# Folding the second model's weights with three products of f16 halves instead of one in fp32, with a redrawn order

## The chip, the cores and the metric

The kernel runs on one core of a Trainium2 chip. The metric is device time in microseconds (us). The kernel before takes 1667.03 us (median of three runs, 1666.88 to 1668.13). The core has five instruction streams: PE (matrix products, with weight loads that can run beside them), DVE (vector work), ACT (activations and scaled copies), POOL (general vector work without access to the accumulators) and SP (which here issues all DMAs).

## The reference

Two attention models on separate inputs, whose outputs are put side by side. Both have 2048 positions, width 1024 and 32 heads of 32.

```python
def _A_ref(x, wq, wk, wv, wo, beta):        # four segments of 512
    q, k, v = x @ wq, x @ wk, x @ wv          # by head
    ...
    for s in range(N):
        p = softmax(qs @ ks.T * scale + mask); a_dot = p @ vs
        a_mem = (phi(qs) @ M) / (phi(qs) @ z + 1e-6)
        outs.append(g * a_mem + (1 - g) * a_dot)
        M, z = M + phi(ks).T @ vs, z + phi(ks).sum()
    return o @ wo

def _B_ref(x, wqkv, w_phi, wo):
    qkv = (x @ wqkv) ...
    pq = einsum("bhsd,hdf->bhsf", q, w_phi)   # per head, 32 by 32
    pk = einsum("bhsd,hdf->bhsf", k, w_phi)
    phi_q = concat(softmax(pq), softmax(-pq))
    phi_k = concat(softmax(pk), softmax(-pk))
    kv, z = einsum(phi_k, v), phi_k.sum()
    o = (phi_q @ kv) / (phi_q @ z + 1e-6)
    return o @ wo

return concatenate([_A_ref(...), _B_ref(...)], axis=-1)
```

In the second model q and k enter only through q @ w_phi and k @ w_phi. So the kernel multiplies w_phi into the weights once: wqkv's q and k columns, head by head, times the head's 32x32 feature map. That is the fold.

## The kernel before, in words

**Precision.** Nearly all products run in f16. A matrix is scaled by its own maximum and split into an upper half (the value rounded to f16) and a lower half (the rest, f16 again); a product is then three matmuls, upper by upper, upper by lower and lower by upper. A split is a scaled copy on ACT and a subtraction on DVE or POOL (`halves`, `forms`).

**Stages.** From the start to about 43 us the first segment of the first model and its first weights are loaded, scaled and split. Then 32 units of the first model's attention follow (`produce(u)`, `attend(u)` and the shared `values(u)`): projections of a head group, row maxima, scores, masks, values and the memory. Alongside, unit by unit, the second model's weights are prepared: `fold` in the units, `sizes_v` and `weights_v` for its value weights. From about 805 us the second model runs, first its keys and values (to about 1180 us), then its queries and output, with the first model's output weights prepared meanwhile; the last eight blocks, from about 1520 us, are the first model's output projection.

**The fold** (L1135 to L1221). The feature map stands in a tile of its own, `phib` (128 x 8 x 128, fp32): eight groups of four heads, each a 128x128 matrix with the four 32x32 maps on its diagonal and zeros elsewhere. POOL clears it at L1110 (after all other clears) and four DMAs at L1112 fill the diagonals. The q and k weights are eight blocks (m = 0 to 7) of four parts of 128x512. Block 0 is folded at the start, in `fold(-1)`: four fp32 matmuls a part (L1180). The other 28 parts are folded one per unit: a DMA loads the part into a stage buffer `st` (tag st, two buffers, L1147), four fp32 matmuls of 128 columns multiply it with `phib` (L1214), and DVE scales the result into the block `quad` (L1217). `size` (L1150) loads the parts of the next block into the same two buffers and takes its largest absolute row sums on ACT (L1156); with the feature map's own sums (`phs`, L1117) they bound the folded weights and give the scale `sif`. After the fourth part, `cut` builds seven sums and differences of the block, splits them and writes them to DRAM.

**The order.** Every instruction is written down as an operation with an engine, a duration, what it reads and writes, and a priority (`op`, L143). `run` (L207) then fixes the order of all engines by playing the operations through: at each step the engine that can start first takes the ready operation with the smallest priority. [...] Where PE would wait long, filler matmuls whose result nobody uses are put in (`fill`, L194, seen as L379 in the profile). `nudge` (L92) shifts the priorities of each run of 60 operations by a hash of a number in the table `NUDGE`, so the table draws one order among many. SP issues DMAs in the order so found; each engine works through its list in order.

**The end.** For each of eight blocks seven groups of twelve matmuls (L1718) fill three accumulators; `keep` (L1727) copies one out on ACT, `store` (L1739) adds another on DVE and sends it with a DMA (L1744). The last is a copy of 128x512 on ACT and one DMA of 256 KB.

Of the kernel before, what the change touches and what calls it, by code (L numbers as in the profile page):

```python
# [8 lines left out]
F32 = mybir.dt.float32  # L9
F32R = mybir.dt.float32r  # L10
F16 = mybir.dt.float16
# [34 lines left out]
NUDGE = {0: 820989, 2: 102852, 3: 529656, 4: 266905, 5: 924189, 6: 435410, 9: 911235, 12: 450738, 13: 124130, 14: 669972,  # L46
# [261 lines left out]
def tile_kernel(ctx: ExitStack, tc: tile.TileContext, ax, aw, awv, awo, beta, bx, bwqk, bwv, bphi, bwo, out):  # L308
# [65 lines left out]
    for t in vlb:  # L374
        nc.gpsimd.memset(t[:, :, :, 32:33], 0.0)
        nc.gpsimd.memset(t[:, :, :, 65:66], 1.0)
# [758 lines left out]
    def fold(n, prio, dep=()):  # L1135
# [14 lines left out]
        def size(m, i, qd=None):  # L1150
            if i == 0:
                sizes[m] = (G.buf("a", [128, 4], F32, "twf", 1), G.buf("a", [128, 2], F32, "sif", 2))
# [648 lines left out]
```

## Time and profile before

| what | us |
|---|---|
| median of the runs | 1667.03 |
| the profiled execution | 1667.0 |
| its span, first to last instruction | 1665.2 |
| POOL busy | 1060.6 |
| ACT busy | 1111.6 |

The profile is of one execution. "Busy" of an engine is the time that its instructions take by the trace; a matmul's end is modelled, and neighbouring matmuls overlap, so distances from start to start tell more about PE than durations. A row of a group gives the line, the engine, the operation, output and inputs, the shapes and how many there were, then the busy time, the mean of one in ns, and the idle time of the engine before them with what ended it.

### The profile page before, as it was taken

What the parts mean: (1) busy time and instruction counts of PE and PEld (TensorE: products, weight loads), DVE (VectorE), ACT (ScalarE), POOL (GpSimd) and SP (SyncE); (2) the same over time, 40 slices, a digit from 0 to 9 for tenths busy, and PEclk for the clock granted to TensorE, in tenths of its full rate; (3) what the DMA queues carried; (4) which work ended last, traced back from release to release, by engine and by line L of the source; (5) the groups of instructions that cost most, each with busy time, mean ns of one, the idle gap of its engine ahead of it and who ended that gap; (6) DMA issues with size and microseconds to landing.
All of it is one profiled execution on the core that took longest, in us unless ns stands there. A gap on an engine that the chain in (4) does not pass through costs nothing.

```text
span 1665.2 us, 35567 instructions
## 1 busy us (share of the span) xinstructions
PE 1644.1 (99%) x12922; PEld 964.4 (58%) x12922; DVE 1357.2 (82%) x3212; ACT 1111.6 (67%) x2044; POOL 1060.6 (64%) x1393
## 2 busy tenths in 40 slices
PE   8999999999999999999999999999999999999999
PEld 6666667667676666766754444445544444444444
DVE  6899989899897888897877898988997786975441
ACT  8798779868787777777865767645755464454431
POOL 4967577577777886967874454546699897640000
PEclk9999999999999999999999999999999999999999
DMA  7845556779456462756566354276466665753311
GB/s 238 238 137 155 158 156 170 204 203 240 115 160 163 132 180 90 193 194 176 154 203 260 121 197 170 85 257 248 171 153 152 169 176 158 216 149 136 121 57 64
DMA packets 265455, 279.68 MB, mean 168 GB/s; under 512 B 162752, under 2 KB 215744, under 8 KB 256704
## 3 DMA queue, kind: packets, MB, share of 16 engines
q1 hardware_dynamic: 265280, 277.42, 56.1%
q8 instruction: 101, 1.65, 0.4%
q14 instruction: 74, 0.61, 0.1%
HBM read 143.34 MB, written 85.00 MB: 137 GB/s over the span
## 4 chain that ended last, share of the span: by engine, by line
PE 80%; DVE 10%; ACT 3%; POOL 3%; issue 2%; DMA 1%; SPq 0%; DVEq 0%; ACTq 0%; POOLq 0%
PE proj L421 25%; PE proj L617 14%; PE misc L421 10%; PE proj L1718 5%; PE s L1033 4%; PE pv L1069 4%; PE s L940 3%; PE s L617 3%; PE s L1718 2%; PE misc L617 2%; PE pv L1654 2%; PE misc L1718 1%; PE misc L1214 1%; DVE mx L1319 1%; DVE s L946 1%
## 5 line engine op out<-in xcount | busy, mean ns | idle before, releaser
L421 PE MATMUL proj<-S,S 128*128 128x512 f16 (+1 forms) x2304 | 494.1, 343 | 0.7 <-ACT S L448 0.2
L421 PEld LDWEIGHTS <-S 128*128 128x128 f16 x3072 | 288.1, 98 | 160.4 <-issue 0.8
L617 PE MATMUL proj<-S,S 128*128 128x512 f16 x1488 | 342.7, 379 | 6.7 <-ACT cs L623 5.7
L617 PEld LDWEIGHTS <-S 128*128 128x128 f16 x1968 | 186.9, 98 | 219.9 <-issue 7.5
L1046 POOL TENSOR_SCALAR_AFFINE_SELECT ph<-ph 128x256 f16<-128x256 f16 (+1 forms) x448 | 194.9, 458 | 109.8 <-DVE ph L1040 93.1
L1040 DVE SCALAR_TENSOR_TENSOR ph<-s,ph 128x512 f16<-128x512 f32 x320 | 208.6, 684 | 51.0 <-ACT ph L1039 45.1
L946 DVE CUSTOM_DVE_ANT_0 s<-s,causal 128x384 f32<-128x384 f32 (+3 forms) x512 | 241.3, 510 | 8.6 <-PE s L940 6.1
L1039 ACT ACTIVATE ph<-s 128x512 f16<-128x512 f32 x320 | 185.4, 647 | 0.7
L421 PE MATMUL misc<-S,ot 128*128 128x512 f16 x768 | 171.0, 379 | 0.0
L1326 ACT ACTIVATE e<-e,sk 128x256 f32<-128x256 f32 x256 | 114.3, 498 | 62.1 <-DVE e L1323 39.8
L421 PEld LDWEIGHTS <-ot 128*128 128x128 f16 x768 | 73.9, 98 | 88.3
L1037 ACT ACTIVATE s<-s,bdl 128x512 f32<-128x512 f32 x160 | 105.7, 702 | 21.6 <-PE s L1033 21.4
L1037 ACT ACTIVATE s<-s,bd 128x512 f32<-128x512 f32 x160 | 102.9, 688 | 21.0 <-PE s L1033 20.4
L1033 PE MATMUL s<-S 104*128 104x512 f16 (+3 forms) x512 | 113.2, 299 | 0.1
L940 PE MATMUL s<-S 96*128 96x512 f16 (+3 forms) x512 | 112.0, 299 | 0.7 <-DVE dm L993 0.3
L421 PE MATMUL proj<-wv,S 128*128 128x256 f16 x768 | 101.2, 272 | 0.0
L1069 PEld LDWEIGHTS <-ph 128*128 128x128 f16 x2560 | 88.8, 96 | 18.9 <-POOL ph L1046 0.8
L1623 POOL TENSOR_TENSOR e<-e,zb 128x512 f32<-128x512 f32 x64 | 85.1, 1344 | 16.2 <-DVE r L1329 13.2
L1069 PE MATMUL pv<-vl,ph 128*128 128x66 f16 (+1 forms) x2560 | 92.2, 184 | 0.0
L1329 DVE TENSOR_REDUCE r<-e 128x32 f32<-128x1024 f32 x64 | 76.6, 1205 | 12.3 <-ACT e L1326 12.0
L617 PE MATMUL s<-S,S 128*128 128x512 f16 x324 | 78.5, 379 | 0.4 <-DVE S L450 0.4
L946 DVE DVE_READ_ACCUMULATOR2_ANT mt<- 128x1 f32 x512 | 72.1, 141 | 0.0
(373 smaller groups left out, 3299.8 us busy)
## 6 DMA issues: line engine op xcount, KB each, us to landing
S<-h SPq DMA_DIRECT2D x192, 128.0 KB
S<-wf_d SPq DMA_DIRECT2D x21, 1024.0 KB
st<-bwqk SPq DMA_DIRECT2D x56, 256.0 KB
wf_d<-fo SPq DMA_DIRECT2D x48, 256.0 KB
out<-os SPq DMA_DIRECT2D x39, 256.0 KB
wf_d<-oT SPq DMA_DIRECT2D x36, 256.0 KB
S<-xf_d SPq DMA_DIRECT2D x9, 1024.0 KB
S<-aw SPq DMA_DIRECT2D x16, 512.0 KB
```

Source lines behind the costliest of these rows:

```text
L421: op(PE, dur, lambda c=c, a=a, b=b, lv=lv, rv=rv: nc.tensor.matmul(pv(), lv(), rv(), start=(c == 0 and a + b == 0), stop=(c == n - 1 and a ...
L617: op(PE, 0.2165, lambda n=n, a=a, b=b, lv=lv, rv=rv: nc.tensor.matmul(ps(), lv(), rv(), start=(start and n == 0 and a + b == 0), stop=(n = ...
L940: nc.tensor.matmul(ps()[:, o:o + 128 * i + 128], st()[0:96, 0, h, 128 * i:128 * i + 128], st()[0:96, 1, h, 0:128 * i + 128], start=True, s ...
L946: dve({128: 0.216, 256: 0.381, 384: 0.6, 512: 0.648}[n], lambda h=h, i=i, o=o, n=n: nc.vector.tensor_tensor_reduce(ps()[:, o:o + n], ps()[ ...
L1033: nc.tensor.matmul(ps()[:, o:o + n], st()[0:104, 1, h, 128 * j:128 * j + 128], st()[0:104, 0, h, 128 * j:512], start=True, stop=True)
L1037: act(0.571, lambda: nc.scalar.activation(ps(), ps(), AF.Exp, bias=0.0, scale=bd()[:, 4, i2, 0:1]), r=[(bd, i2)], w=[ps])
L1039: act(0.478, lambda: nc.scalar.activation(ph()[:, 0], ps(), AF.Copy, scale=2.0 ** 14), r=[ps], w=[(ph, 0)])
L1040: dve(0.6, lambda: nc.vector.scalar_tensor_tensor(ph()[:, 1], ps(), 2.0 ** 14, ph()[:, 0], op0=OP.mult, op1=OP.subtract), r=[ps, (ph, 0)], ...
L1046: nc.gpsimd.affine_select(pd, pd, pattern=[[0, n], [1, 128]], compare_op=OP.is_ge, fill=0.0, base=0, channel_multiplier=-1)
L1069: nc.tensor.matmul(ps()[:, i, n0:n1], ph()[:, a, o:o + 128], vl()[:, j, h4 + h, n0:n1], start=(i == 0 and a == 0), stop=(j == min(i, 2)), ...
L1326: op(ACT, 0.41, lambda i=i: nc.scalar.activation(e()[:, 4 * i:4 * i + 4], e()[:, 4 * i:4 * i + 4], AF.Exp, bias=0.0, scale=sk()[:, i:i + 1 ...
L1718: op(PE, 0.2165, lambda n=n, a=a, b=b: nc.tensor.matmul(ps(), v(a)[:, n, :], wform[w]()[:, b, n, :], start=(start and n == 0 and a + b == ...
```

## The change

- **The fold in halves.** The feature map is scaled and split once into `phh` (128 x 2 x 8 x 128, f16; a scale on `phf`, one ACT pass and one DVE pass over 128x1024). Each of the 28 parts is scaled in place on ACT, its upper half is written by ACT and its lower half by POOL into the place of `quad` that the result takes later. Twelve f16 matmuls (three products for each of four column blocks) then stand where four fp32 ones did. DVE's scaled copy follows as before. Block 0 stays in fp32.
- **Sizes.** `size` finds the block's own maximum beside the bound of the folded block, so its two scales come from one matmul with two columns; two or three tiny DVE instructions are added per block.
- **The feature map's tile** is now a view of one of the slots (S14, first used for the attention of unit 2), cleared first of POOL's larger clears; the two value tiles and `mem` are cleared behind it.
- **The last copy** is shared: ACT takes the first 256 columns, DVE the other 256, and two DMAs of 128 KB store them.
- **The order**: a new table `NUDGE`; four kinds of small DVE instructions are marked `port`, and two durations are changed (no instruction changes by that, only the order).

```diff
-    phib = G.buf("a", [128, NG, 128], F32, "phib")
-    op(POOL, 1.19, lambda: nc.gpsimd.memset(phib(), 0.0), w=[phib], prio=-1)
+    PK = [(stk[2], (0, r)) for r in range(7)]
+    phh, phf = G.buf("a", [128, 2, NG, 128], F16, "phh"), G.buf("a", [128, 3], F32, "phf")
...
+    nc.gpsimd.memset(phib(), 0.0)
+    for t in (x() for x in vlb):
+        nc.gpsimd.memset(t[:, :, :, 32:33], 0.0)
+        nc.gpsimd.memset(t[:, :, :, 65:66], 1.0)
+    op(POOL, 1.19, lambda: nc.gpsimd.memset(mem, 0.0), w=[memb, *PK], prio=-1)
...
+    scale((phf, lambda: phf()[:, 2:3]), 1, (phf, None, phf), 0.7)
+    op(ACT, 1.04, lambda: nc.scalar.activation(phh()[:, 0], phib(), AF.Copy, scale=phf()[:, 1:2]), r=[phf, *PK[:4]], w=[(phh, 0)], prio=0.8)
+    op(DVE, 1.25, lambda: nc.vector.scalar_tensor_tensor(
+        phh()[:, 1], phib(), phf()[:, 1:2], phh()[:, 0], op0=OP.mult, op1=OP.subtract),
...
-        for c in range(4):
-            op(PE, 0.23, lambda c=c: nc.tensor.matmul(ps()[:, c, :], st()[:, c * 128:(c + 1) * 128], phib()[:, g, :],
-                                                      start=True, stop=True), r=[st, phib], w=[ps], prio=prio, need=[qd])
         k = 2 * q + hb
-        op(DVE, 0.663, lambda: nc.vector.tensor_scalar(qd()[:, k], ps().rearrange("p c n -> p (c n)"), si()[:, 1:2], None, op0=OP.mult),
+
+        def wh():
+            return qd()[:, k].bitcast(F16).rearrange("p (a n) -> p a n", a=2)
+
+        op(ACT, 0.53, lambda: nc.scalar.activation(st(), st(), AF.Copy, scale=si()[:, 1, 1:2]), r=[si], w=[st], prio=prio)
+        op(ACT, 0.53, lambda: nc.scalar.activation(wh()[:, 0], st(), AF.Copy), r=[st], w=[(qd, k)], prio=prio)
+        op(POOL, 1.12, lambda: nc.gpsimd.tensor_tensor(wh()[:, 1], st(), wh()[:, 0], op=OP.subtract), r=[st], w=[(qd, k)], prio=prio)
+
+        def f():
+            for c in range(4):
+                for a, b in ((0, 0), (0, 1), (1, 0)):
+                    nc.tensor.matmul(ps()[:, c, :], wh()[:, a, c * 128:(c + 1) * 128], phh()[:, b, g, :],
+                                     start=(a + b == 0), stop=(a == 1))
+
+        op(PE, 0.65, f, r=[(qd, k), phh], w=[ps], prio=prio, need=[qd])
+        op(DVE, 0.663, lambda: nc.vector.tensor_scalar(qd()[:, k], ps().rearrange("p c n -> p (c n)"), si()[:, 0, 0:1], None, op0=OP.mult),
...
         op(DVE, 0.172, lambda zr=zr, v=v: nc.vector.tensor_scalar(zr(), za()[:, v], 1e-12, None, op0=OP.max),
-           r=[(za, (hb, 0)), (za, (hb, 1))], w=[zr], prio=P)
+           r=[(za, (hb, 0)), (za, (hb, 1))], w=[zr], prio=P, port=True)
...
         mult(X, "A22", "T4", False)
-        store(keep(X, "os", 1), c + 8, 0)
+        o = G.buf("stage", [128, 512], F32, "os", 1)
+        op(ACT, 0.33, lambda: nc.scalar.activation(o()[:, 0:256], X()[:, 0:256], AF.Copy, scale=wsc[:, 2, 1, 0:1]),
+           r=[X, (wscs, (2, 1))], w=[(o, 0)], prio=P)
+        op(DVE, 0.37, lambda: nc.vector.tensor_scalar(o()[:, 256:512], X()[:, 256:512], wsc[:, 2, 1, 0:1], None, op0=OP.mult),
+           r=[X, (wscs, (2, 1))], w=[(o, 1)], prio=P)
+        for h in range(2):
+            op(SP, 0.6, lambda h=h, r=128 * (c + 8): nc.sync.dma_start(
+                out[r:r + 128, 256 * h:256 * h + 256], o()[:, 256 * h:256 * h + 256]), r=[(o, h)], prio=P, lat=1.5)
```

What the change moves is shown at three places. The first is PE at the first fold of block 1, in the fourth unit or so. Before, the fold (L1214) stands between a projection of the first model (L421) and the row maxima and scores of two units (L940, L1033):

```order
L421 LDWEIGHTS S_1673
L421 MATMUL proj<-S_261,S_1673 128x512
L1214 MATMUL misc<-phib,st 128x128 x4
L940 LDWEIGHTS S_127
L940 MATMUL s<-S_127 128x512
L1033 LDWEIGHTS S_136
L1033 MATMUL s<-S_136 128x256
```

After, at the same place (L419, L1099 and L1250 are the projection, the transpose of a unit's output and the fold):

```order
L419 MATMUL proj<-S_235,S_1691 128x512
L1099 MATMUL misc<-ident,osum 128x128 x4
L419 LDWEIGHTS S_1691
L419 MATMUL proj<-S_235,S_1691 128x512
L1250 LDWEIGHTS quad
L1250 MATMUL misc<-phh,quad 128x128
```

The last two rows stand there twelve times in a row, then the scores (L1031) follow. The four matmuls have become twelve pairs that read `quad`, which ACT and POOL have to fill first, instead of the loaded part.

The second place is SP at the start. Before (aw, ax, awv are weights and input of the first model, bwqk the second model's, bphi the feature map):

```order
L468 DMA S_133<-aw 128x1024
L468 DMA S_138<-ax 128x512 x2
L1112 DMA phib<-bphi 32x8x32 x2
L468 DMA S_138<-ax 128x512 x2
L468 DMA S_162<-ax 128x512 x4
L1174 DMA quad<-bwqk 128x512
L1112 DMA phib<-bphi 32x8x32
```

After:

```order
L466 DMA S_132<-aw 128x1024
L466 DMA S_137<-ax 128x512 x2
L1120 DMA S_121<-bphi 32x8x32 x2
L466 DMA S_137<-ax 128x512 x2
L466 DMA S_161<-ax 128x512 x4
L466 DMA S_132<-aw 128x1024
L466 DMA S_183<-awv 128x2048
L1199 DMA quad<-bwqk 128x512 x4
L1120 DMA S_121<-bphi 32x8x32 x2
```

The first two loads of the feature map stay in third place; the weights aw and awv are now issued ahead of block 0's four parts and of the feature map's last two loads.

The third place is PE a little later, where block 0's sixteen fp32 matmuls now stand. Before, they are spread over four places, the first two of them inside the first projection, eight matmuls of the sixteen:

```order
L379 MATMUL fill<-ident 128x128 x5
L421 LDWEIGHTS S_160
L421 MATMUL proj<-S_239,S_160 128x512
L1180 MATMUL kv<-phib,quad 128x128 x4
L421 LDWEIGHTS S_160
L421 MATMUL proj<-S_239,S_160 128x512
```

After, all sixteen stand together, inside the second projection, twelve of whose products are of the first half of the segment (S_235) and twelve of the second (S_257):

```order
L419 MATMUL proj<-S_235,S_159 128x512
L1205 MATMUL kv<-S_121,quad 128x128 x16
L419 LDWEIGHTS S_159
L419 MATMUL proj<-S_235,S_159 128x512
L419 LDWEIGHTS S_159
L419 MATMUL proj<-S_257,S_159 128x512
```

Fillers (x5 and so on) stand at six places before, 5, 5, 3, 2, 3 and 3 matmuls, the second at 57 us, the third at 846 us and the last three between the keys and the queries of the second model; after, at seven places, 5, 2, 3 and 2 before the value projection begins, and 3, 4 and 3 between keys and queries.

More of the change, by code (lines that the diff above doesn't have):

```diff
@@ L371, in tile_kernel @@
     mem = ca.tile([128, NG, 132], F32, name="mem")
-    nc.gpsimd.memset(mem, 0.0)
     vlb = [ca.tile([128, 4, 8, 66], F16, name=f"vl{i}") for i in range(2)]
-    for t in vlb:
-        nc.gpsimd.memset(t[:, :, :, 32:33], 0.0)
-        nc.gpsimd.memset(t[:, :, :, 65:66], 1.0)
     G = Graph(pools)
@@ L1113, in tile_kernel @@
             phib()[32 * r:32 * r + 32, :, 32 * r:32 * r + 32],
-            view(bphi, r * 1024, [[32, 32], [4096, NG], [1, 32]])), w=[(phib, r)], prio=-3, lat=1.5, kb=64)
+            view(bphi, r * 1024, [[32, 32], [4096, NG], [1, 32]])), w=[PK[r]], prio=-3, lat=1.5, kb=64)
     for g in range(NG):
         op(DVE, 0.2, lambda g=g: nc.vector.tensor_reduce(
-            phs[:, g:g + 1], phib()[:, g, :], axis=AX.X, op=OP.add, apply_absolute_value=True), r=[phib], w=[(phss, g)], prio=0.6)
+            phs[:, g:g + 1], phib()[:, g, :], axis=AX.X, op=OP.add, apply_absolute_value=True), r=PK[:4], w=[(phss, g)], prio=0.6)
+    op(DVE, 0.07, lambda: nc.vector.tensor_reduce(phf()[:, 2:3], phs, axis=AX.X, op=OP.max),
+       r=[(phss, g) for g in range(NG)], w=[phf], prio=0.7)
+    scale((phf, lambda: phf()[:, 2:3]), 1, (phf, None, phf), 0.7)
+    op(ACT, 1.04, lambda: nc.scalar.activation(phh()[:, 0], phib(), AF.Copy, scale=phf()[:, 1:2]), r=[phf, *PK[:4]], w=[(phh, 0)], prio=0.8)
+    op(DVE, 1.25, lambda: nc.vector.scalar_tensor_tensor(
+        phh()[:, 1], phib(), phf()[:, 1:2], phh()[:, 0], op0=OP.mult, op1=OP.subtract),
+       r=[phf, (phh, 0), *PK[:4]], w=[(phh, 1)], prio=0.8, port=True)
     quads, sizes = {}, {}
```

37 lines of the change are left out of this document (27 added, 10 removed), and 32 rows, old and new, of the table NUDGE.

## The prediction

> **What bounds the kernel now.** I read the page first, for which engine leaves no time over, then the busy time by stretches, for whether that holds everywhere, then the timeline at one place, for what the changed work costs there.
>
> ```profile
> span 1665.2 us, 35567 instructions
> PE 1644.1 (99%) x12922; PEld 964.4 (58%) x12922; DVE 1357.2 (82%) x3212; ACT 1111.6 (67%) x2044; POOL 1060.6 (64%) x1393
> ...
> PE 80%; DVE 10%; ACT 3%; POOL 3%; issue 2%; DMA 1%; SPq 0%; DVEq 0%; ACTq 0%; POOLq 0%
> ```
>
> These are lines of the page: the span, the busy time of the engines, and the chain that ended last by engine. The next are three of the stretches: length, then busy time of PE, weight loads, DVE, ACT and POOL, the granted clock and the DMA share.
>
> ```profile
> 43.00:149.00 106.00, 105.88 (x917) 69.41 (x916) 99.05 (x301) 89.69 (x161) 81.81 (x127) 1.00 0.60 170
> 149.00:805.00 656.00, 653.50 (x6211) 447.19 (x6210) 572.44 (x1716) 512.05 (x934) 489.79 (x728) 1.00 0.62 169
> 1180.00:1222.00 42.00, 36.64 (x279) 21.14 (x278) 41.46 (x75) 24.33 (x57) 30.09 (x35) 1.00 0.56 151
> ```
>
> PE is busy 653.50 of 656 us in the stretch from 149 to 805, which holds all 28 folds that the change rewrites, at the full clock (1.00). The chain that ended last lies on PE for 80%. So a microsecond of PE taken out there shortens the run, as long as no other engine turns late. The next is DVE: 572.44 of 656 is 87%, ACT 78%, POOL 75%. The one stretch where PE really waits is 1180 to 1222, the passage from the keys to the queries of the second model: 5.4 us idle of 42.
>
> **The fold itself.** These rows are the timeline of PE around the first fold and near the end (start, length, line, operation), and the group of the fold's matmuls.
>
> ```profile
> 148.73 0.81 PE L421 MATMUL proj<-S,S 128*128 128x512 f16 x3
> 149.38 1.05 PE L1214 MATMUL misc<-phib,st 128*128 128x128 f32 x8
> 150.26 0.38 PE L940 MATMUL s<-S 96*128 96x512 f16 x1
> ...
> 150.71 0.89 PE L1006 MATMUL misc<-vl,pkt 128*128 128x132 f16 x12
> 151.43 0.60 PE L1033 MATMUL s<-S 104*128 104x512 f16 x3
> ...
> 1645.50 2.75 PE L1718 MATMUL misc<-S,ot 128*128 128x512 f16 x12
> 1648.09 2.75 PE L1718 MATMUL proj<-S,ot 128*128 128x512 f16 x12
> ```
>
> ```profile
> L1214 PE MATMUL misc<-phib,st 128*128 128x128 f32 x224 | 32.7, 281 | 0.8 <-DVE ph L1040 0.8
> ```
>
> A matmul's own duration (281 ns) is mostly latency, so I count from start to start. A fold is four fp32 matmuls, which leave eight records: 149.38 to 150.26 is 0.88 us. There are 224 records, so 28 folds: 24.6 us. The new fold is twelve f16 matmuls of 128 columns, each with its own weight load. No such group is in the trace; its neighbours are two. L1006 is also twelve f16 matmuls with a fresh 128x128 weight each, in the same pattern of halves, with 132 columns: 150.71 to 151.43 is 0.72 us, 0.060 each. The 512-column group takes 1648.09 - 1645.50 = 2.59 us for twelve, 0.216 each, and a quarter of that is 0.054. So a fold costs between 12 x 0.054 = 0.65 and 0.72 us. I take 0.057, between the two, or 0.68 us: 28 x (0.88 - 0.68) = **5.5 us less**, with 4.5 and 6.4 as ends.
>
> [...]
>
> **What the fold adds on other engines.** Each fold gains two ACT passes over 128x512 (a scaled copy in place, then the upper half) and one subtraction on POOL. Their nearest kin:
>
> ```profile
> 36.40 2.55 ACT L1191 ACTIVATE quad<-quad,sif 128x512 f32<-128x512 f32 x4
> L527 ACT ACTIVATE fo<-quad 128x512 f16<-128x512 f32 x32 | 21.4, 668 | 7.1 <-DMA wf_d<-fo 4.1 <-POOL quad L520 2.9
> L528 POOL TENSOR_TENSOR fo<-quad,fo 128x512 f16<-128x512 f32 x32 | 37.6, 1175 | 10.4 <-ACT fo L527 10.3
> L1321 DVE TENSOR_TENSOR e<-proj,mx x32: 624/680/685, 927.2 to 1465.4; 128x512 f32<-128x512 f32 x32
> L1321 DVE TENSOR_TENSOR e<-cs,mx x16: 673/732/1976, 905.8 to 1453.9; 128x512 f32<-128x512 f32 x16
> ```
>
> ACT: 28 x (0.64 + 0.67) = 36.7 us more, which takes it from 512 to 549 of 656 us (84%). POOL: 28 x 1.175 = 32.9 us more, from 490 to 523 (80%). DVE: the sizing of each of eight blocks gains two tiny instructions, some 2.5 us in all, and the feature map's split one pass; it stays near 88%. None of this is on PE's path by itself. What is: the fold's matmuls waited only for a DMA and now wait for DMA, ACT, ACT, POOL in a row. Queued behind a late fold on PE is everything, since PE works in order. The two stage buffers of the loaded blocks are also held from the landing to POOL's subtraction instead of to the matmuls, so the next load on SP, and the transfers of the halves (S<-h) queued behind it, can start later. The present wait of PE for fold inputs is 0.8 us in total (the L1214 row). With 4 to 6 points more load on ACT and POOL I put **1 us more** stalls; the ends are 0 and 4 (5 folds of 28 each late by most of a 1.175 us subtraction).
>
> POOL's work also presses on DVE: a DVE tensor_tensor that reads two SBUF tiles (e<-cs,mx) takes up to 1976 ns where the same one with PSUM input never passes 685. [...] For the sum it stays within the 0 to 4 us.
>
> **The start.** Everything up to about 43 us is paced by ACT, which makes the first segment's halves.
>
> ```profile
> 1.47 1.06 POOL L372 MEMSET mem<- 128x1056 f32 x1
> ...
> 2.86 1.27 POOL L1110 MEMSET phib<- 128x1024 f32 x1
> 3.09 1.07 DVE L369 COPY sel<-hd 128x4 f32<-128x4 f32 x1
> ...
> 4.16 0.83 SPq L1112 DMA_DIRECT2D phib<-bphi  x2
> 4.39 4.24 ACT L658 ACTIVATE S<-sel 8x512 f16<-8x512 f32 x8 [2.33 <-DVE sel L370]
> ...
> 8.66 1.06 ACT L490 ACTIVATE S<-S 128x1024 f16<-128x1024 f32 x1
> ...
> 15.25 4.40 ACT L448 ACTIVATE S<-S,xsc 128x512 f16<-128x512 f32 x7
> ...
> 24.24 1.28 PE L1180 MATMUL kv<-phib,quad 128*128 128x128 f32 x10
> 24.26 1.90 ACT L490 ACTIVATE wv<-S 128x2048 f16<-128x2048 f32 x1
> ...
> 31.27 4.75 PE L421 MATMUL proj<-wv,S 128*128 128x256 f16 x42
> ...
> 57.24 1.38 PE L379 MATMUL fill<-ident 128*128 128x128 f32 x10
> 58.68 0.39 PE L421 MATMUL proj<-S,S 128*128 128x512 f16 x1
> ```
>
> Clearing the feature map's tile first (where mem is cleared now, at 1.47 instead of 2.86) lets its DMAs and the six segment loads behind them go up to 1.4 us earlier. It hardly helps: the gate is ACT, which fills the index rows from 4.39 to 8.63 and begins the weights' size at 8.66 without a pause. DVE's sel copy, which lets ACT start, sat out POOL's clear (3.09 to 4.16); with the clears in another order it ends between 3.4 and 4.2, so 0 to 0.7 us are gained. Against this, the sixteen fp32 matmuls of the first block, which now fill PE's pauses between 16 and 27 us, all stand behind the second projection's eleventh matmul. I follow the rows: ACT needs 8 x 0.63 from 15.25, so 20.3, then 1.06 for one size and 1.90 for the other, then 0.63 for a half; PE enters the second projection near 24.0, spends 24 x 0.216 = 5.2 us there and 16 x 0.22 = 3.6 us on the fp32 matmuls (1.28 us for ten records, two to a matmul), and reaches the value projection near 32.8 instead of 31.3. That is 1.5 us late. But the five fillers (ten records) from 57.24 to 58.68, 1.4 us in which PE had nothing to do, are gone from the order; I count 1.2 of them as won back. **Net: 0.3 us more**, from -1 to +2.
>
> **The passage to the queries.** [...]
>
> ```profile
> PE proj L617 <- ACT cs L623: 5.7, 3, 2.4
> ```
>
> ```profile
> 1187.37 1.09 DVE L1510 TENSOR_SCALAR zr<-zr,osc 128x8 f32<-128x8 f32 x1
> ...
> 1221.62 1.72 DVE L1567 TENSOR_TENSOR wsc<-wsc,osc 128x1 f32<-128x1 f32 x1
> ```
>
> The first row is PE's longest sum of waits in all; the others are the timeline of DVE. [...] The new order still has fillers there, ten matmuls for eight, so it expects pauses too. I take **1 us less**, from -4 to +3: the whole order is drawn anew, and the same kind of wait can fall elsewhere.
>
> **The end.**
>
> ```profile
> 1658.45 2.75 PE L1718 MATMUL proj<-S,h 128*128 128x512 f16 x12
> ...
> 1661.29 0.69 ACT L1735 ACTIVATE os<-proj,wsc 128x512 f32<-128x512 f32 x1 [7.13 <-PE proj L1718]
> 1662.00 0.33 SPq L1744 DMA_DIRECT2D out<-os  x1
> ```
>
> ```profile
> L1326 ACT ACTIVATE e<-e,sk 128x256 f32<-128x256 f32 x256 | 114.3, 498 | 62.1 <-DVE e L1323 39.8 <-DVE e L1321 17.0 <-DVE wsc L434 4.9
> ```
>
> The last copy falls from 0.69 to about 0.50 us (256 columns), with DVE on the other half; but the second store is issued about 0.4 us after the first (0.83 for two, above), so it leaves 0.2 us later than the single one now and carries half the bytes. **0.2 us less**, between -0.6 and +0.2.
>
> **The sum**, against the profiled execution (1667.0 us, its span 1665.2 and 1.8 around it; the median of the three runs is 1667.03, the same): 1667.0 - 5.5 + 1.0 + 0.3 - 1.0 - 0.2 = **1661.6 us**, 0.32% less. A measurement of this kernel can tell about 0.2% from no change: under 1663.7 is faster, over 1670.4 slower.
>
> **The rivals.**
> - *The gain is spent again* (1663.7 to 1670.4). PE's 5.5 us are freed, but DVE at 87% and a longer chain ahead of each fold give 4 us back: 1661.6 + 4 = 1665.6. For it: DVE is busy 93% from 43 to 149 us (99.05 of 106). Against it: in 656 us PE waited 2.5 us under these loads. 23%.
> - *The fold arrives late* (slower). PE stands before L1250 for POOL's subtraction. From 5.5 / 28 = 0.2 us a fold the gain is gone, and from (5.5 + 3.3) / 28 = 0.31 us the run is slower by over 0.2%. If 11 of the 28 folds wait for one subtraction of 1.175 us, that is 13 us: 1661.6 - 1.0 + 13 = 1673.6. Against it: the order puts other matmuls between a fold's subtraction and its products. 8%.
> - *Weight loads set the pace* (slower).
>
> ```profile
> L421 PEld LDWEIGHTS <-S 128*128 128x128 f16 x3072 | 288.1, 98 | 160.4 <-issue 0.8 <-ACT S L448 0.7 <-POOL S L445 0.3
> ```
>
>  A weight load lasts 98 ns. If twelve did not overlap, a fold would take 1.18 us and the folds 28 x 0.3 = 8.4 us more than now: 1661.6 + 5.5 + 8.4 = 1675.5. The pairs of L1006 at 0.060 us speak against it. 2%. [...]
> - *The order wins more than the fold does*: the passage's pauses fall by 4 of their 5.4 us. 1667.0 - 5.5 + 1.0 + 0.3 - 4 - 0.2 = 1658.6. 15%.
>
> My forecast (1660 to 1663.7) has the remaining 52%. Together: faster 52 + 15 = 67%, within 0.2% 23%, slower 8 + 2 = 10%. The range of 8 in 10 runs from 1656.5, below the better order, to 1668.5, inside the spent gain.
>
> **What would show it.** In the changed profile the fold's 336 matmuls (L1250) should stand 0.054 to 0.060 us apart, and PE's busy time should fall by about 5 us. ACT and POOL should be busier by some 37 and 33 us. PE's waits for quad (L1245) should stay below 2 us in all; 5 us or more would make the second rival right. The value projection should begin near 33 us, later than now, and the stretch from the end of the keys to the first queries should be idle for 3 to 5 us. Wrong would be: equal PE busy time, or fold pairs at 0.08 us.

## The result, and the profile after

The changed kernel takes 1682.22 us (median of 5, 1681.49 to 1683.38), before takes 1667.03 (1666.16 to 1668.13) beside it: a ratio of 1.0085 with a 95% interval of 1.0074 to 1.0096. It is slower by 15 us where 5.4 less were forecast, and lies outside the range.

The first rows are the page of the changed kernel: span, busy time by engine, and the chain that ended last by engine.

```profile
span 1680.3 us, 35939 instructions
PE 1650.1 (98%) x13038; PEld 962.0 (57%) x13038; DVE 1377.0 (82%) x3233; ACT 1144.2 (68%) x2101; POOL 1091.8 (65%) x1421
...
PE 56%; DVE 12%; POOL 5%; ACT 3%; issue 2%; DVEq 0%; ACTq 0%; POOLq 0%
```

ACT is busy 32.6 us more and POOL 31.2 more, as the sum had it (37 and 33). The chain lies on PE for 56% instead of 80%. PE's busy time rose by 6.0 us (1644.1 to 1650.1), where the prediction expected some 5 less; its own work became less all the same, as is worked out below. The next rows are the timeline of PE at the first fold (start, length, line, operation), the group of the fold's matmuls, and PE's waits for the split.

```profile
150.76 0.83 PE L1250 MATMUL misc<-phh,quad 128*128 128x128 f16 x12
151.42 0.38 PE L1031 MATMUL s<-S 104*128 104x256 f16 x2
```
```profile
L1250 PE MATMUL misc<-phh,quad 128*128 128x128 f16 x336 | 23.6, 219 | 0.2 <-POOL quad L1245 0.2
```

Twelve products take 151.42 - 150.76 = 0.66 us, 0.055 each, and PE waits for POOL's subtraction 0.2 us in the whole run. So the fold itself is as fast as forecast, and is not late.

The time went into waits elsewhere. The rows are stretches of before, then of the change: length, busy PE, weight loads, DVE, ACT, POOL, granted clock, DMA share.

```profile
50.00:800.00 750.00, 747.37 (x7029) 508.79 (x7028) 660.12 (x1976) 596.48 (x1083) 560.78 (x840) 1.00 0.61 169
800.00:1350.00 550.00, 541.14 (x3814) 277.58 (x3811) 477.43 (x854) 349.49 (x686) 371.37 (x394) 1.00 0.57 183
```
```profile
50.00:800.00 750.00, 744.53 (x7142) 501.86 (x7140) 664.64 (x1971) 625.29 (x1134) 590.50 (x866) 1.00 0.62 168
800.00:1350.00 550.00, 532.81 (x3712) 272.38 (x3710) 475.31 (x853) 339.22 (x664) 355.78 (x384) 0.99 0.54 178
```

All folds of the change but the last lie in the first stretch (the last starts at 812.09 us). There PE's idle time grows from 2.6 to 5.5 us; in the second, with that one fold at its beginning, from 8.9 to 17.2 us.

Busy time hides short waits and a slow clock, so I also took, for each matmul, the time from its start to the next one's start, less the median of its line and shape in before (for the two lines that before lacks, the fold's L1250 and a scale's L1185, less their own median in the run). What is left are mostly waits and slow clock; I call it **lost time**. Over the run it is 20.0 us before and 40.8 in the change, while the medians themselves sum to 1639.2 and 1633.3: 20.9 more lost, 5.8 less work, together the 15 by which the spans differ. The measure is for differences: the matmuls of one line (L1654, after 1220 us) alternate between some 4 and 52 ns, its median is put at 52, and so the last stretch comes out below zero in both kernels. The fold alone takes 25.1 us before and 18.8 in the change by its medians, 6.3 less; from start to start, with the waits that follow its products, it is 27.5 and 19.5.

Two places show what such waits are, both after 800 us. First a late burst of score groups of the first model: stretches of the change (columns as above), and then the nearest of before.

```profile
826.00:836.00 10.00, 8.18 (x107) 4.91 (x104) 6.77 (x13) 10.00 (x21) 7.99 (x16) 1.00 0.38 119
836.00:844.00 8.00, 6.64 (x42) 4.52 (x41) 7.10 (x16) 8.00 (x17) 5.10 (x10) 0.57 0.60 220
```
```profile
836.00:840.00 4.00, 4.00 (x39) 2.15 (x38) 4.00 (x7) 4.00 (x9) 1.64 (x3) 1.00 0.68 163
840.00:844.00 4.00, 4.00 (x56) 2.62 (x55) 4.00 (x8) 1.43 (x4) 3.60 (x8) 1.00 0.21 82
```

In the change ACT has no pause for 18 us (10.00 of 10, 8.00 of 8), and PE runs dry behind it. From 824 to 844 us ACT does 14 of the softmax's exponentials (L1035, in before L1037):

```profile
L1035 ACT ACTIVATE s<-s,bdl 128x512 f32<-128x512 f32 x14 | 9.7, 745 | 0.0
```
```profile
L1037 ACT ACTIVATE s<-s,bdl 128x512 f32<-128x512 f32 x8 | 5.4, 723 | 1.0 <-PE s L1033 1.0
```

The second row is before, from 828 to 848 us: 8 of them, mixed with the second model's work. None of the fold's ACT passes is among them (the last starts at 802.5 us).

The second place is the keys of the second model. The rows are the timeline of PE in the change and in before (start, length; in brackets the idle time before it and what ended it).

```profile
981.26 2.54 PE L615 MATMUL s<-S,S 128*128 128x512 f16 x11
985.52 0.23 PE L1510 MATMUL kv<-ot,pt 128*128 128x65 f16 x2 [1.72 <-ACT pt L1500]
986.39 0.48 PE L1510 MATMUL kv<-ot,pt 128*128 128x65 f16 x10 [0.63 <-DVE pt L1503]
```
```profile
983.25 2.10 PE L617 MATMUL s<-S,S 128*128 128x512 f16 x9
985.19 1.33 PE L1473 MATMUL kv<-ot,pt 128*128 128x65 f16 x36
986.36 0.81 PE L617 MATMUL s<-S,S 128*128 128x512 f16 x3
```

In the change the products of keys and values (L1510) are next in order before ACT and DVE have made `pt`, and PE stands 1.72 and 0.63 us; in before they follow at once. The same code, two orders.

### The profile page after: what moved, and what is told of

It is laid out like the page before. It is cut to its first block, busy times and chain, and to the rows that moved or that the text cites. A ratio compares the mean times of both kernels' runs of the same rounds, so it can differ in the third digit from the quotient of the medians.

```text
span 1680.3 us, 35939 instructions
## 1 busy us (share of the span) xinstructions
PE 1650.1 (98%) x13038; PEld 962.0 (57%) x13038; DVE 1377.0 (82%) x3233; ACT 1144.2 (68%) x2101; POOL 1091.8 (65%) x1421
## 4 chain that ended last, share of the span: by engine, by line
PE 56%; DVE 12%; POOL 5%; ACT 3%; issue 2%; DVEq 0%; ACTq 0%; POOLq 0%
PE proj L419 13%; PE proj L615 12%; PE misc L419 7%; PE proj L1755 5%; PE s L615 3%; PE s L1755 2%; PE s L1031 2%; PE pv L1067 2%; PE s L938 2%; PE misc L615 1%; DVE s L944 1%; PE misc L1755 1%; DVE mx L1356 1%; DVE r L1366 1%; PE pv L1691 1%
## 5 line engine op out<-in xcount | busy, mean ns | idle before, releaser
L419 PE MATMUL proj<-S,S 128*128 128x512 f16 (+1 forms) x2304 | 503.2, 343 | 0.1
L419 PEld LDWEIGHTS <-S 128*128 128x128 f16 x3072 | 286.9, 98 | 157.5 <-issue 0.8
L615 PE MATMUL proj<-S,S 128*128 128x512 f16 x1488 | 344.9, 380 | 4.3 <-ACT cs L621 2.3
L615 PEld LDWEIGHTS <-S 128*128 128x128 f16 x1968 | 187.4, 98 | 217.8 <-issue 6.0
L944 DVE CUSTOM_DVE_ANT_0 s<-s,causal 128x512 f32<-128x512 f32 (+3 forms) x512 | 241.8, 508 | 8.9 <-PE s L938 6.3
L1037 ACT ACTIVATE ph<-s 128x512 f16<-128x512 f32 x320 | 187.2, 647 | 1.0
L419 PE MATMUL misc<-S,ot 128*128 128x512 f16 x768 | 170.9, 379 | 0.0
L419 PEld LDWEIGHTS <-ot 128*128 128x128 f16 x768 | 74.2, 98 | 88.9
L1031 PE MATMUL s<-S 104*128 104x512 f16 (+3 forms) x512 | 114.8, 299 | 3.2 <-DVE oall L1071 1.5
L1035 ACT ACTIVATE s<-s,bdl 128x512 f32<-128x512 f32 x160 | 106.0, 703 | 17.4 <-PE s L1031 17.3
L1035 ACT ACTIVATE s<-s,bd 128x512 f32<-128x512 f32 x160 | 105.5, 698 | 17.6 <-PE s L1031 11.2
L1660 POOL TENSOR_TENSOR e<-e,zb 128x512 f32<-128x512 f32 x64 | 89.6, 1417 | 26.3 <-DVE r L1366 20.7
L419 PE MATMUL proj<-wv,S 128*128 128x256 f16 x768 | 101.8, 272 | 0.0
L615 PE MATMUL s<-S,S 128*128 128x512 f16 x324 | 77.8, 379 | 0.0
L1503 POOL TENSOR_TENSOR pt<-e,pt 128x512 f16<-128x512 f32 x40 | 49.0, 1235 | 39.8 <-ACT pt L1500 39.6
```

The costliest lines, as they stand in the source:

```text
L419: op(PE, dur, lambda c=c, a=a, b=b, lv=lv, rv=rv: nc.tensor.matmul(pv(), lv(), rv(), start=(c == 0 and a + b == 0), stop=(c == n - 1 and a ...
L615: op(PE, 0.2165, lambda n=n, a=a, b=b, lv=lv, rv=rv: nc.tensor.matmul(ps(), lv(), rv(), start=(start and n == 0 and a + b == 0), stop=(n = ...
L944: dve({128: 0.216, 256: 0.381, 384: 0.6, 512: 0.648}[n], lambda h=h, i=i, o=o, n=n: nc.vector.tensor_tensor_reduce(ps()[:, o:o + n], ps()[ ...
L1031: nc.tensor.matmul(ps()[:, o:o + n], st()[0:104, 1, h, 128 * j:128 * j + 128], st()[0:104, 0, h, 128 * j:512], start=True, stop=True)
L1035: act(0.571, lambda: nc.scalar.activation(ps(), ps(), AF.Exp, bias=0.0, scale=bd()[:, 4, i2, 0:1]), r=[(bd, i2)], w=[ps])
L1037: act(0.478, lambda: nc.scalar.activation(ph()[:, 0], ps(), AF.Copy, scale=2.0 ** 14), r=[ps], w=[(ph, 0)])
```

## The experiments

Each ratio is to before on the same chip, whose median there was 1667.3 to 1668.6 us. Two kinds of edits recur. A table is "numbered as in" another kernel when operations that the other lacks get no number and no shift. An order is "written out" when, in place of priorities, a list fixes which operation comes next on each engine.

### 1. Tables: is it the order or the load?

```diff
-NUDGE = {0: 688381, 4: 803830, ...
+NUDGE = {}
```

> The changed code with an empty table, so that the planner follows its priorities alone; nothing is left out of the computation. To be read against the next run, the old code with an empty table, since in neither has a table been chosen for the code. Theory 'order': the fold in halves takes some 8 us of PE's work off (27.5 to 19.5 us of fold matmuls in the two traces) and the 23 us more of waits and half clock come from the new order; then this kernel is 3 to 13 us faster than the next one. Theory 'load': the two ACT copies and the POOL subtract of each of 28 parts starve PE in any order; then this kernel is 10 to 20 us slower than the next one. Either way both may lie well above 1667 us.

> The code of before with an empty table. Theory 'order': 3 to 13 us slower than the run above. Theory 'load': 10 to 20 us faster than the run above. What it lies above 1667 us is what before's table is worth to before's code; I expect 5 to 25 us.

```diff
-        o.base, o.at = prio, len(self.ops)
+        o.base, o.at = prio, -1 if self.uncounted else self.no
+        self.no += not self.uncounted
```

> The changed code with before's table, and its operations numbered as in before: the new ones get no number and no shift, so every operation that both kernels have gets the shift that it had in before. Theory 'order' in its simple form (the old table is good, the new one bad): 1655 to 1666 us. Theory 'load': 1676 to 1690 us whatever the table. Third theory, 'fit' (a table is worth something only to the very code it was chosen for, since any new operation sends the plan elsewhere): 1670 us or more here too, and the trace would show other places of waiting than the changed kernel's.

> The code of before with the table of the change, numbered as in the changed kernel, so that each operation gets the shift that it has there. Theory 'order': the bad order without the gain, 1682 + 8 = 1690 us (1682 to 1698). Theory 'load': without the load the time is that of before, 1660 to 1672 us. Theory 'fit': 1675 us or more, about what the empty table gives.

Measured, with the end that the planner itself gives to the program (what it returns when all is laid out):

| code | table | planner's end, us | measured, us | ratio, 95% |
|---|---|---|---|---|
| before | its own | 1680.7 | 1667.0 | 1 |
| change | its own | 1679.6 | 1682.2 | 1.0085 (1.0074 to 1.0096) |
| change | empty | 1728.1 | 1741.6 | 1.0443 (1.0426 to 1.0461) |
| before | empty | 1723.7 | 1735.1 | 1.0409 (1.0386 to 1.0431) |
| change | before's | 1735.7 | 1742.2 | 1.0449 (1.0433 to 1.0464) |
| before | the change's | 1703.9 | 1706.5 | 1.0232 (1.0217 to 1.0247) |

A table is worth about 60 us to the code it belongs to (68 for before, where I had expected 5 to 25, and 59 for the change). On the other code, even with every common operation shifted as there, before's table is worth nothing and the change's 29 us. "Order" in its simple form fell (the change with before's table should have come under 1667), and so did "load" in full (before's code with the change's table should have been at 1667). "Fit" is nearest, though the change's table on before's code should by it have given no more than the empty one. With empty tables the changed code is 6.5 us slower than before's, good to about 5 us: neither the 3 to 13 us faster of "order" nor the 10 to 20 slower of "load". A change that meets a table cannot be read apart from it.

### 2. The smallest change: marks alone

The code and the table are before's; of the change only the planner's marks are taken. The eight small DVE reductions of `bdm` are planned at 0.15 us instead of 0.071 and marked `port=True`, and five small DVE operations late in the program (four on `zr`, one on `wsc`) are marked too. The planner starts a marked DVE operation only when the POOL operation that it placed last is over, and a POOL operation only when the last marked one of DVE is.

```diff
-        op(DVE, 0.071, lambda i=i: nc.vector.tensor_reduce(bdm[:, i, :, 32], ..., w=[(bdmb, i)], prio=0.3)
+        op(DVE, 0.15, lambda i=i: nc.vector.tensor_reduce(bdm[:, i, :, 32], ..., w=[(bdmb, i)], prio=0.3, port=True)
...
-           r=[(oscs, 1)], w=[zr], prio=P)
+           r=[(oscs, 1)], w=[zr], prio=P, port=True)
```

> [...] No instruction is added, taken out or altered; only the plan can move. Theory 'order': one early operation that moves by a tenth of a microsecond sends the whole plan elsewhere, the table no longer fits, and the planner's own end goes from 1680.7 to 1737.1 us: 1725 to 1755 us on the chip. Theory 'load', and every theory by which only the work that is done costs time: 1667 us as before, within 5.

1729.67 us, a ratio of 1.0371 (1.0351 to 1.0390): 62 us more for the same work, fillers aside. The rows are its page and its group of fillers, and then that of before.

```profile
PE 1688.0 (98%) x13126; PEld 995.4 (58%) x13126; DVE 1363.1 (79%) x3212; ACT 1110.9 (64%) x2044; POOL 1057.4 (61%) x1393
```
```profile
L379 PE MATMUL fill<-ident 128*128 128x128 f32 x246 | 33.6, 289 | 1.2 <-DVE za L1482 1.1
```
```profile
L379 PE MATMUL fill<-ident 128*128 128x128 f32 x42 | 6.0, 283 | 0.0
```

DVE, ACT and POOL have the counts of before (3212, 2044, 1393); PE's 204 matmuls more are the 246 fillers in place of 42. What moves is the plan alone: a tenth of a microsecond near the start changes which operation is next all the way down. This is "order" at its plainest.

### 3. Tables found alike for both codes

To compare the codes with tables of equal standing, I searched a table for each in the same way: change the seed of one stretch at random, keep it where the planner's end comes no later, starting once from an empty table and once from the kernel's own.

> The code of before with a new table, found from an empty one by random changes of single stretches that are kept where the planner's own end of the program comes no later; as many changes are tried as for the next kernel. The planner ends it at 1684.3 us (before itself 1680.7, the change 1679.6, the empty tables 1723.7 and 1728.1). Theory 'order': the chip's time strays from the planner's end by the draw, by 10 us or more either way whatever the code (so far -13.7 before, +2.6 the change, +13.5 and +11.4 the empty tables): 1675 to 1695 us. Theory 'load' in full (the 15 us are the fold's): before's code beats its planner's end again by some 14 us: 1668 to 1673 us.

> The changed code with a table found in the same way with the same effort; the planner ends it at 1687.2 us, 2.9 us after the run above. If the fold's 8 us less of PE work are spent on its own waits (the two runs at the written-out order: about 6.5 us of load), this kernel stands within some 5 us of the run above once the planner's 2.9 us are taken off. Theory 'load' in full: 15 us or more above the run above. 1680 to 1697 us.

> The code of before, its own table taken on by the same kind of changes until the planner ends 4.1 us earlier, at 1676.6 us. If the planner's end were the chip's time up to a constant, 1663 us; if before's 1667 us is a draw that the planner did not foresee (theory 'order'), moving many stretches loses part of it: 1667 to 1680 us.

> The changed code, its own table taken on in the same way until the planner ends 3.7 us earlier, at 1675.9 us. Up to a constant: 1678 us. Theory 'order': a new draw, as likely better as worse by a few us more: 1671 to 1686 us. Theory 'load' in full: nothing below 1678 us.

| start of the search | code | planner's end | measured, us | ratio, 95% |
|---|---|---|---|---|
| empty | before | 1684.3 | 1693.26 | 1.0154 (1.0139 to 1.0169) |
| empty | change | 1687.2 | 1692.54 | 1.0151 (1.0136 to 1.0166) |
| its own | before | 1676.6 | 1676.16 | 1.0053 (1.0038 to 1.0068) |
| its own | change | 1675.9 | 1675.72 | 1.0048 (1.0032 to 1.0065) |

With tables found alike the change makes 0.7 and 0.4 us less: nothing that can be told from zero. These are one table for each code and start, and the draws scatter by more than that, so a gain or a loss of a few us could hide in them. "Load" in full fell again: by it before's code should have come to 1668 to 1673 us, and the change nowhere below 1678. And before's 1667 us is not its code's but its table's: the planner promises 4.1 us off, and the chip gives 9 more. The change's own table, taken on for 3.7 us, gains 6.5. Over these kernels the chip strays from the planner's end by -13.7 to +13.5 us.

### 4. The change's order held, fold and split varied

```diff
-        op(ACT, 0.53, lambda: nc.scalar.activation(st(), st(), AF.Copy, scale=si()[:, 1, 1:2]), ...
-        op(ACT, 0.53, lambda: nc.scalar.activation(wh()[:, 0], st(), AF.Copy), ...
-        op(POOL, 1.12, lambda: nc.gpsimd.tensor_tensor(wh()[:, 1], st(), wh()[:, 0], op=OP.subtract), ...
+        op(ACT, 0.53, lambda: nc.scalar.activation(qd()[:, k], st(), AF.Copy), ...
...
+            op(PE, 0.23, lambda c=c: nc.tensor.matmul(ps()[:, c, :], qd()[:, k, c * 128:(c + 1) * 128], phh()[:, g, :], ...
```

> The order of the changed kernel is written out and kept on every engine; only the fold is undone in it: one ACT copy brings a part to the quad, four fp32 matmuls fold it from there, the second ACT operation and the POOL subtract of each part are gone, and the feature map is kept in fp32. It prices the fold's PE term at a fixed order. If PE's work counts in full (theories 'order' and 'fit'), the eight us that the trace of the change shows at the fold (27.5 us before, 19.5 after) come back: 1682 + 8 = 1690 us (1687 to 1693). If the change is slow because of the POOL subtract and the second copy (theory 'load'), taking them away gives more than the fp32 matmuls cost: under 1682 us, down to 1672.

1684.50 us, 1.0091 (1.0076 to 1.0106): as slow as the change, and neither the 1687 or more of one theory nor the 1682 or less of the other. So the fold in halves, as a whole, gains nothing that shows at this order; the microseconds of PE's work that it saves and a POOL pass and an ACT pass per part weigh about the same.

The next five take the two apart; where the split is on 4 columns, or fp32 matmuls read the two halves, the folded weights come out wrong, and the runs tell of time alone. The split on 4 columns:

```diff
-        op(POOL, 1.12, lambda: nc.gpsimd.tensor_tensor(wh()[:, 1], st(), wh()[:, 0], op=OP.subtract), ...
+        op(POOL, 0.15, lambda: nc.gpsimd.tensor_tensor(wh()[:, 1, 0:4], st()[:, 0:4], wh()[:, 0, 0:4], op=OP.subtract), ...
```

With 4 columns split, the matmuls take one column, repeated, as their weights. The matmuls in fp32, with all of the split kept:

```diff
-                for a, b in ((0, 0), (0, 1), (1, 0)):
-                    nc.tensor.matmul(ps()[:, c, :], wh()[:, a, c * 128:(c + 1) * 128], phh()[:, b, g, :], ...
+                nc.tensor.matmul(ps()[:, c, :], qd()[:, k, c * 128:(c + 1) * 128], phh()[:, g, :], start=True, stop=True)
```

> The same written-out order, with the fold's twelve f16 matmuls as in the change, but the two ACT operations and the POOL subtract of each part run on 4 of their 512 columns, so that some 0.5 us of ACT twice and 1 us of POOL per part are gone and every wait and place in the queues stays; the matmuls repeat one column of each four as their weights, which leaves the folded weights wrong. It prices the split's load and its chain at a fixed order. Theory 'load': 28 parts of some 2 us less, 10 us or more faster than the change, 1662 to 1672 us. Theories 'order' and 'fit': the order was laid out with the split in it, ACT and POOL are not what the waits of the change stand at, so within 3 us of the change: 1679 to 1683 us.

1677.26 us, 1.0049 (1.0032 to 1.0066), by the two ratios 0.36% or 6 us below the change. The other four ran beside one another, in more rounds:

> The changed kernel itself, once more on the chip of the next three runs, so that the four stand beside one another: twelve f16 matmuls or four fp32 ones to a part, the split on all columns or on 4 of 512, all in the order of the change. 1682 to 1684 us.

> The change's order written out, the split of each part kept whole (both ACT operations, the POOL subtract), but the fold's twelve f16 matmuls replaced by four fp32 ones on the same tile, which reads the bytes of the two halves as fp32, so the folded weights are wrong. Only PE's work goes up, by the 8 us of the two traces (27.5 against 19.5 us). If PE's work counts in full at this order: 8 us above the changed kernel, 1690 us. If part of it fills waits: 2 to 6 us above.

> The kernel with the split on 4 columns once more, beside the changed kernel on one chip and with more rounds. Theory 'load' at its measured size: 4 to 8 us below the changed kernel. If the first reading was the start's chance (its trace has 2.2 us less before the first big matmuls, where no split runs): 3 to 5 us below.

> Both at once in the change's order: the split on 4 columns, and four fp32 matmuls in the place of the twelve (one column of each repeated as weights; folded weights wrong). If PE's 8 us and the split's load simply add: the changed kernel + 8 - 6, some 2 us above it. If the split's cost is there only because PE got faster (the split's end is what the faster fold then waits for): no more than 1 us below the run with fp32 and the whole split.

| fold, split | measured, us | ratio, 95% | lost time 50 to 800 us | 800 to 1350 us |
|---|---|---|---|---|
| f16, whole (the change) | 1683.91 | 1.0095 (1.0082 to 1.0109) | 19.7 | 23.7 |
| fp32, whole | 1686.81 | 1.0110 (1.0095 to 1.0126) | 16.3 | 24.7 |
| f16, 4 columns | 1676.13 | 1.0051 (1.0038 to 1.0063) | 15.2 | 23.1 |
| fp32, 4 columns | 1682.12 | 1.0084 (1.0070 to 1.0098) | 12.4 | 22.1 |
| before, in its order | 1667.87 | 1 | 12.1 | 7.6 |

A difference of two such medians is good to about 3 us (two half intervals of 0.14%, added as squares: 0.20% of 1667). PE's work on the fold, 6.3 us by its medians, is worth 2.9 us with the whole split and 6.0 with the small one: with the split in place about half of what the fold frees seems to be waited away at once, though the 3.4 us that are missing hardly exceed the 3. The split costs 7.8 us under the fast fold and 4.7 under the slow one, so it is not only the faster fold that makes it cost, as one reading of the last expectation would have it. From the slow fold without the split to the change it is 1.8 us more. The last columns show where, each from one execution (those of the second and third row are the slowest of theirs, 2.4 and 3.2 us above the median): the lost time of the first stretch follows the fold and the split, from 12.4 to 19.7 us; that of the second stands at 22 to 25 whatever they do. Those some 15 us over before's 7.6 are not the work of the fold or the split.

### 5. Before's order from 811 us on

`RANK` gives each operation its place: the change's if the change's plan starts it before 811 us, else before's, behind all those. In the second run the table searched on from the change's own stands for the change, up to 808 us.

```diff
+RANK = _order(
...
-            o = min(some, key=lambda x: x.prio)
+            o = queues[e].pop()
```

> The changed code, whole and with nothing left out, in an order written out: that of the change for everything that its plan starts before 811 us (all 28 folds but their last evictions), and from there the order of before, on every engine. In the trace of the change the waits before 800 us are 7 us more than in before and those between 800 and 1350 us some 15 us more; PE's fold work is 8 us less. If the loss is in the order after 800 us, where no fold runs: 1683 - 14 + 1 for the seam = 1670 us (1666 to 1675). If the fold's work is what is late there (buffers, transfers or the clock that it leaves behind): 1678 us or more.

> The changed code again, with the order of the run 'searched on' (1675.7 us) up to 808 us of its plan and before's from there: the version that the runs point to, if any beats before's 1667 us. From the two traces, the waits between 800 and 1350 us would fall by about 11 us: 1675.7 - 11 + 1 for the seam = 1665.5 us (1662 to 1671); at the most 5 us under before, as likely not to be told from it.

The first takes 1673.88 us, 1.0040 (1.0027 to 1.0054); the second 1670.88 us, 1.0024 (1.0015 to 1.0032), 5 us above the 1665.5 expected. These are the stretches of the first, to be set beside those of the change:

```profile
50.00:800.00 750.00, 742.68 (x7121) 500.52 (x7120) 662.59 (x1965) 623.30 (x1131) 587.70 (x863) 1.00 0.62 168
800.00:1350.00 550.00, 539.46 (x3808) 276.37 (x3806) 478.83 (x866) 347.11 (x680) 370.84 (x392) 1.00 0.56 182
```

The same code, all of it, is 8 to 10 us faster than the change (1682.2 and 1683.9 us in its two sets of runs) on nothing but another order of what comes after the folds. PE's idle time there falls from 17.2 to 10.5 us, its lost time from 24.3 to 10.7. The slow clock of the change in this stretch (last section) is gone too (1.00 in the second row); by the lengths and the half clock measured there it can be at most (6.8 + 3.4) / 2 = 5.1 of these us, an estimate. Whatever the folds leave behind them, it does not hold before's order up for more than some 3 us. The second kernel is the fastest found of the changed code, and still slower than before; none found beats before.

## Why the prediction was wrong, step by step

- **The fold's matmuls**: right. Forecast 0.68 us a fold, measured 0.66; 28 x (0.88 - 0.66) = 6.2 us of PE's work instead of 5.5. A pair stands 0.055 us from the next, where 0.08 was to show the forecast wrong; by the fold's own 0.88 us, the gain would be gone from 0.88 / 12 = 0.073 on, an estimate. But "a microsecond of PE taken out there shortens the run", on condition that no other engine turns late, held only without the split's load (6.0 us); with it, 2.9 us came through.
- **The extra stalls**: 1 us, with ends 0 and 4, was mis-sized. The split's load costs 4.7 to 7.8 us. I looked for it at the fold, where PE would stand before L1250; it waits 0.2 us there. The cost is spread over other lines, as ACT and POOL, 28.8 and 29.7 us busier from 50 to 800 us, are late for everybody: lost time with the fast fold is 15.2 us without, 19.7 with it. That the load makes them late is argued from these sums; no single wait shows it. Fold and split together come to +1.8 us, good to 3 either way, at a fixed order, and the changed code to -0.7 and -0.4 with tables found alike and +6.5 with empty ones. So "the gain is spent again", the first rival, comes nearest to what the change does by itself.
- **The order**: this step failed, and with it the sign. The prediction put the redrawn order into one place, "1 us less, from -4 to +3", the passage to the queries. There it was even too careful. No run shows this 1 us by itself: the run with the marks alone is 62 us slower. What the traces show in its place are the five instructions on `zr` and `wsc` that the change marks, on one to eight columns each. In before, three of them take 0.97, 1.09 and 1.72 us, and each ends within 0.03 us after a POOL instruction that runs beside it; the other two take 0.16 and 0.22. In the change the five take 0.13 to 0.73 us. The passage comes some 15 us later there (the last product of keys and values starts at 1201.8 us, before at 1185.2), so the stretch to set beside 1180 to 1222 us of before is this one:

```profile
1195.00:1237.00 42.00, 39.57 (x295) 22.46 (x294) 41.90 (x77) 27.85 (x59) 31.18 (x35) 1.00 0.45 139
```

 PE's idle time in these 42 us fell from 5.4 to 2.4, and the waits of L615 for ACT's `cs`, over the whole run, from 5.7 to 2.3. But the table sets the order of all 14,800 operations, and from 800 to 1350 us the new order loses 16.7 us more than the old. The run with before's order from 811 us on shows 8 to 10 us of it. What it still is above before: 6.2 us more lost time from 50 to 800 us (18.3 against 12.1) against 4.5 us less work in the whole run, and 3.1 us more behind the seam (10.7 against 7.6).
- **The fold arrives late**, the rival for the other sign: it did not. The run was slower by more than this rival's price, without its mechanism.
- **The start**: 0.3 us more. The value projection begins at 34.35 us, 3.1 later than before, instead of 1.5 later; the fillers at 57 us are gone as forecast; lost time up to 50 us is 6.8 instead of 6.5.

```profile
27.61 3.73 PE L1205 MATMUL kv<-S,quad 128*128 128x128 f32 x32
...
34.35 0.49 PE L419 MATMUL proj<-wv,S 128*128 128x256 f16 x3
```

- **The end**: 0.2 us less was wrong in its mechanism, though small. The halves of the last copy do not run side by side:

```profile
1675.63 0.59 PE L1755 MATMUL proj<-S,h 128*128 128x512 f16 x2
1676.26 0.48 DVE L1805 TENSOR_SCALAR os<-proj,wsc 128x256 f32<-128x256 f32 x1 [1.84 <-PE proj L1755]
1676.78 0.89 SPq L1808 DMA_DIRECT2D out<-os  x2
1676.83 0.47 ACT L1803 ACTIVATE os<-proj,wsc 128x256 f32<-128x256 f32 x1 [7.65 <-DVE os L1805]
```

 ACT's half waits for DVE's, so the copy lasts from 1676.26 to 1677.30, 1.04 us instead of 0.69. From the last matmul's end to the span's end it is 4.1 us, as before (4.0).
- **The range and chances**: all my rivals kept the quality of the order and moved one wait; one case, the order as a whole, was missing, though both tables stood in the diff.

What stays open: how before's table came to beat its planner's end by 13.7 us, which no table found here repeats; how the 6 us that are left in the run with before's later order divide between order, seam and fold; and what the slow clock (below) costs by itself, since no run took it away alone.

## What to carry to other kernels

Where a planner with a tuned table sets the order, time the code and the table apart: the old code with the new table, and both codes with tables found with equal effort; here the code made between 0.7 us less and 6.5 us more over three pairs of tables, the table 60, and marks that add no work 62. A saving on the bound engine counts only as far as the engines that feed it are not loaded in exchange: some 6 us of PE were paid for with 29 us each on ACT and POOL, at a price that showed nowhere near the edit. An engine that waits 0.2 us at the edited line is no sign that the edit is free.

## What the hardware showed that I had not expected

Before runs at the full granted clock up to its last products (1.00 from 0 to 1660 us). In the change the clock is 0.57 of full from 836 to 844 us (row above) and 0.72 in the next row, right behind the two places where PE ran dry:

```profile
982.00:986.00 4.00, 2.03 (x11) 0.71 (x9) 4.00 (x7) 1.56 (x4) 0.00 (x0) 1.00 0.00 0
986.00:992.00 6.00, 5.61 (x54) 3.63 (x55) 5.04 (x13) 4.79 (x10) 5.94 (x5) 0.72 0.90 288
```

In finer stretches it is 0.50 from 836.9 to 843.7 us, 6.8 us, and from 987.1 to 990.5 us, 3.4 us, the one twice the other, and 1.00 in the 0.4 us or more just before and just behind each. What makes it drop is not shown: PE was busy for 8.18 of the 10 us and 2.03 of the 4 us ahead, so it had not stood still throughout. At the start of the run the change has a third slow stretch (0.50 from 10.9 to 14.3 us, 3.4 us again), and before has none after an emptier pause (1.00 from 10 to 16 us; the first row is before, the others the change):

```profile
8.00:10.00 2.00, 0.14 (x2) 0.14 (x2) 0.00 (x0) 1.95 (x5) 0.00 (x0) 1.00 0.87 297
8.00:10.00 2.00, 0.39 (x5) 0.20 (x3) 0.00 (x0) 1.95 (x5) 0.00 (x0) 1.00 1.02 331
10.00:12.00 2.00, 2.00 (x14) 2.00 (x15) 1.70 (x5) 2.00 (x4) 1.19 (x1) 0.72 1.03 420
```

In the second execution of the change (the fourth experiment's) the clock is 0.64 from 836 to 844 us, behind 10 us of which PE was busy for 9.07.

In the first of the two places, from 826 to 844 us, ACT was full to the end of the slow stretch, so the clock followed the starving there. From 840 to 843.7 us PE was then busy without a pause at the slow clock (3.70 of 3.70 us, at 0.50), so it may have cost time of its own; how much is not shown.
